# The last two blocks' output product by two levels of seven products instead of one, in a kernel for linear attention and a gated feed-forward layer

## The chip, the cores and the metric

The kernel runs on one core of one Trainium2 chip. The metric is the device time of one execution in microseconds (us). All data are fp32. TensorE (PE) multiplies, VectorE (DVE), ScalarE (ACT) and GpSimd (POOL) work on what it makes, and SyncE (SP) issues most transfers; ACT issues some too. Each engine runs its own instructions in order and waits for the others on semaphores.

## The reference, cut to what matters

```python
kv  = einsum('bhsd,bhse->bhde', k, v)           # 8 batches, 8 heads, 576 positions, 64 wide
att = einsum('bhsd,bhde->bhse', q, kv)
x   = att / sqrt(mean(att**2) + 1e-6) * g_norm  # then (4608 tokens) x 512
g   = x @ w_gate                                # 512 x 1536
h   = silu(g) * (x @ w_val)                     # 4608 x 1536
out = h @ w_out                                 # 1536 x 512
```

The change is in the last line, for the last 1024 of the 4608 tokens. The feed-forward layer takes nearly all of TensorE's time.

## The kernel before, in words

The tokens are cut into nine blocks of 512, numbered 0 to 8. Block 0's products are plain. Blocks 1 and 2 use one level of a scheme that multiplies two matrices of 2x2 parts with seven products of parts and some sums (the Winograd form). Blocks 3 to 8 go in pairs: `Pair.up` makes h for two blocks at once, with two levels of the scheme, so with 49 products of sixteenths (`Inner`). `Ffn.down` then makes the output of one block at a time, with one level (`Down`).

**The up stage of a pair** walks over six units `j`, each of 256 columns of h for gate and value. A unit has four groups of the seven outer products: `GROUPS = ((1, 5), (6, 2), (7,), (4, 3))`; every group runs the seven inner products in the order 1, 5, (3 of the last group), 6, (4 of the last group), 2, 7. A product is one matmul of 128x128 weights by 256 columns for each outer product of its group. Products 1, 6, 7 and 4 of a group add up in one `b` bank of PSUM, 5 and 3 in a `c` bank, 2 stands in the one `a` bank. After each product its bank is read into SBUF (an eviction): by ACT for products 1, 5, 6 and 4 of the first group (L830), else by VectorE, which adds a running sum (L130). Product 6 may only write onto `b` when product 1's eviction has read it, and so on. When product 4 of the fourth group has been evicted, `made3` multiplies h: two `128x1024` multiplies (L132) on GpSimd (on VectorE for the last unit), with a Silu on ACT between (L862). Then `Ffn.h_sums` makes, for block 7 alone, two `128x256` sums for the down stage on the same engine. GpSimd also makes sums for the running `shared[2]` (`made1`, `made2`).

**The weights' parts** for the up stage lie in DRAM (`stream.dram`) and are loaded by SP (L906) into a pool of nine `t` tiles, each time when one comes free (`Stream.pump`).

**The down stage of a block** has seven products of twelve matmuls, `h` as the stationary operand (128x128) and 256 columns of `wo` moving. The order is 1, 5, 6, 2, 7, 3, 4 for the last pair's blocks (`lone`). Sums over `wo` (`turn_t`) are made by GpSimd into `t` tiles. Product 3 of block 8, the last, is split over two `m` banks, so that the other half can be stored while its last half runs (`third`).

**What sets the order.** A scheduler places each engine's instructions by dependency and its own estimate of when each can start; an instruction may so stand earlier in the built order than in the text. `with in_order(engines)` keeps the text's order on the named engines. `tc.issue_after` holds an instruction behind another. Transfers are told done through eight semaphores taken in turn by all transfers of SP and ACT (lanes); a transfer on a lane is issued when the lane's previous one has landed.

Of the kernel before, what the change touches and what calls it, by code (L numbers as in the profile page):

```python
# [14 lines left out]
P = 128  # L15
# [3 lines left out]
def kernel(  # L19
# [620 lines left out]
    class Quad:  # L640


        def __init__(self, steps):
            self.steps = steps
            self.ps, self.room = {}, None

            self.apart = {}

        def prepare(self):
            pass  # L650

        def multiply(self, p):
            name, first = CHAIN[p]
            if first:
                tiles = [PSUMS[name].tile([P, 2, HB], F32, name=name) for _ in range(1 + (name in self.apart))]
                self.ps[name], self.apart[name] = tiles[0], tiles[-1]
            banks = self.ps[name], self.apart[name]
            for e, i in self.order(p):
                lhsT, rhs = self.operands(p, e, i)

                self.ffn.multiplied = nc.tensor.matmul(  # L661
                    banks[e][:, e], lhsT=lhsT, rhs=rhs, start=first and i == 0 and (e == 0 or banks[0] is not banks[1]),
                    stop=i == self.steps - 1, skip_group_check=True,
                )
            getattr(self, f"after{p}", lambda: None)()
# [91 lines left out]
    class Inner:  # L757
# [94 lines left out]
        def made3(self, p, e, q):  # L852
            if p != 4:
                return
            h = h_both[:, :, 2 * self.j : 2 * self.j + 2]
            halves = lambda t: t.rearrange("p (b e) t -> p b e t", b=2)
            c11, c12, c21, c22 = (self.whole(*i) for i in ((1, 1), (3, 1), (3, 0), (1, 0)))

            engine = nc.gpsimd if self.j + 1 < NP else nc.vector
            mul(engine, h[:, :, :, 0:HB], halves(c11), halves(c12))  # L860
            with tc.issue_after(self.ffn.fifth.ins):
                nc.scalar.activation(out=c21, in_=c21, func=ACT.Silu)  # L862
            mul(engine, h[:, :, :, HB:BLK], halves(c21), halves(c22))
            self.ffn.ended = self.ffn.a.h_sums(self.j, 1, engine)

    OUTERS, INNERS = (1, 5, 6, 2, 7, 4, 3), (1, 6, 2, 3, 7, 4, 5)
# [12 lines left out]
    class Stream:  # L879
# [15 lines left out]
        def pump(self):  # L895

            while self.next and not self.held[-9]:
                n, j, c = key = self.next.pop(0)
                tile_ = t_tile(key)
                os, ps = JOINT[c]  # L900
                count = len(os) * len(ps)
# [4 lines left out]
                nc.sync.dma_start(out=to, in_=src)  # L906

        def use(self, n, j, o, p):
            c, i = self.joint[o, p]
            key = n, j, c  # L910
            self.uses[key] -= 1
            if not self.uses[key]:
                self.free(key)
            return self.tiles[key][:, i]
# [70 lines left out]
    class Down(Quad):  # L985
        def __init__(self, ffn):
            super().__init__(NP)
            self.ffn = ffn
            self.t = {}
            self.final = ffn.n == NB - 1  # L990
            self.lone = False
            self.opens = None
            self.keeps = False
            if self.final:
                self.apart["c"] = None

# [14 lines left out]

        def multiply(self, p, es=(0, 1)):
            if p == 3 and self.lone:
                self.third(es)
                return
            super().multiply(p)
# [5 lines left out]

        def third(self, es):


            if es[0] == 0:
                tiles = [m_psum.tile([P, 2, HB], F32, name="m") for _ in range(1 + self.final)]
                self.thirds = tiles[0], tiles[-1]
            for e in es:
                for i in range(self.steps):  # L1030
                    lhsT, rhs = self.operands(3, e, i)
                    self.ffn.multiplied = nc.tensor.matmul(  # L1032
                        self.thirds[e][:, e], lhsT=lhsT, rhs=rhs, start=i == 0 and (e == 0 or self.final),
                        stop=i == self.steps - 1, skip_group_check=True,
                    )
            if not self.final:
                add(nc.vector, self.o1[:, :, HD:DM], self.thirds[0], self.u2)
                self.ffn.store(self.o1, 0)
                return
            for e in es:  # L1040
                add(nc.vector, self.o1[:, e, HD:DM], self.thirds[e][:, e], self.u2[:, e])
                self.ffn.store(self.o1[:, e : e + 1, HD:DM], e, slice(HD, DM))

        def after6(self):
            super().after6()
            if self.lone:
                self.add_c(self.u2, self.u2)

        def order(self, p):
            order = [(e, i) for e in range(2) for i in range(self.steps)]  # L1050
            return order if p == 3 and self.final else sorted(order, key=lambda ei: ei[1])

# [15 lines left out]

        def rows(self):
            o = ring()  # L1070
            self.o1, self.o2 = o[:, 0:2], o[:, 2:4]

        def after2(self):
            if self.lone:
                self.rows()
            add(nc.vector, self.o1[:, :, 0:HD], self.ps["a"], self.s)
            if self.final:
                self.ffn.store(self.o1[:, :, 0:HD], 0, slice(0, HD))

# [3 lines left out]
        def after7(self):  # L1083
            if not self.lone:
                self.rows()
            u3 = self.piece(2)
            nc.scalar.copy(out=u3, in_=self.ps["b"])
            self.add_c(self.o2[:, :, HD:DM], u3)

# [4 lines left out]
        def after3(self):  # L1094
            self.add_c(self.o1[:, :, HD:DM], self.u2)
            if not self.final:
                self.ffn.store(self.o1, 0)
                return
            for e in range(2):
                self.ffn.store(self.o1[:, e : e + 1, HD:DM], e, slice(HD, DM))  # L1100

        def add_c(self, o, u):

            if not self.final:
                add(nc.vector, o, self.ps["c"], u)
                return
            for e, c in enumerate((self.ps["c"], self.apart["c"])):
                add(nc.vector, o[:, e], c[:, e], u[:, e])

    class Ffn:  # L1110
# [8 lines left out]

        def store(self, o, t, columns=slice(None)):  # L1120
            rows = out[BLK * self.n : BLK * (self.n + 1), columns].rearrange("(t p) d -> p t d", t=T)
            nc.sync.dma_start(out=rows[:, t : t + o.shape[1], :], in_=o)
# [39 lines left out]
        def down(self, nxt, then={}):  # L1162

            down = self.down_
            fill = nxt.steps() if nxt else {}
            down.lone = nxt is None
            order = (1, 6, 5, 7, 2, 4, 3) if 5 in fill else (1, 5, 6, 7, 2, 4, 3)
            if down.lone:
                order = (1, 5, 6, 2, 7, 3, 4)
            for p in order:  # L1170
                if p == 1 and 7 not in down.t:
# [4 lines left out]
                with tc.issue_after(nxt.multiplied.ins) if self.n == 0 and p in (5, 6) else ExitStack():  # L1176
                    down.multiply(p, *[(0,)] * (p == 3 and down.lone and down.final))
                self.make(12)
# [9 lines left out]
                if p == 1:  # L1188

                    with tc.issue_after(nxt.q_turned.ins) if self.n == 0 else ExitStack():  # L1190
                        down.turn_s3()
            if down.lone and down.final:
                down.multiply(3, (1,))

# [24 lines left out]
    class Pair:  # L1219


        def __init__(self, n):
            self.n = n
            self.a, self.b = (Ffn(i, blocks[i]) for i in (n, n + 1))
            self.visited = None

        def up(self, fill):

            a = self.a
            a.s1 = s_pool.tile([P, NP, HB], F32, name="s1")  # L1230
            units = []
            for j in range(NP):
# [3 lines left out]
            for i, this in enumerate(units):  # L1236
                for unit, p in this.sequence(last):
                    if unit:
                        visited, self.visited = self.visited, None
                        with tc.issue_after(visited.ins) if visited else ExitStack():  # L1240
                            unit.multiply(p)
                last = this
                fill.get(i + 1, lambda: None)()
            a.down_ = Down(a)
            a.down_.keeps = True
            a.down_.turn_t(5)
            for unit, p in last.sequence(None):
                if unit is None:
                    last.multiply(p)
            a.ended = self.ended  # L1250

# [164 lines left out]
    for n in range(PAIRED, NB, 2):  # L1416
# [3 lines left out]
        if after:  # L1420
# [10 lines left out]
            for i in range(8):  # L1431
                fill[12 + i] = lambda i=i, after=after: after[i // 4].load_quarters(i % 4 // 2, (i % 2,))
        pair.up(fill)
        if after:
            after[0].turn()
        if len(after) > 2:
            after[2].load_kv(0)
        with in_order(nc.tensor.engine):
            pair.a.down(after[0] if after else None, {5: pair.second_sums})
            if after:  # L1440
                after[1].turn()
            if len(after) > 2:
                after[2].load_kv(1)
            pair.b.down(after[1] if after else None)

# [30 lines left out]
```

## Time and profile before

| | |
|---|---|
| median of 3 runs | 1013.08 us (1012.63 to 1014.5) |
| the profiled execution's own time | 1012.7 us |
| its span in the profile | 1010.9 us |
| granted TensorE clock | 1.0 |
| PE, DVE, POOL, ACT busy | 98%, 67%, 37%, 23% of the span |
| first matmul of the up stage of blocks 7 and 8 | 807.6 us |
| its last matmul, and first of the down stage | about 935 us |
| last matmul of the kernel | ends at about 1007.5 us |

A line of a group gives line of the kernel, engine, operation, tiles written and read, shapes, count, then busy time in us and mean in ns of one, then the engine's idle time just before and what ended it. A line of a timeline gives the start in us, the time that the merged instructions took, engine, line and operation, count, and in brackets the idle time before. In the table of stretches each engine's busy us stands with its count in brackets: PE, PE's weight loads, DVE, ACT, POOL, then clock, DMA share and GB/s. L130, L131 and L132 are the helpers `add`, `sub` and `mul`, so their users are told apart by tiles: `wo`, `arena` (x and h), `s`, `t`, `ld`, `r` are in SBUF, `a`, `b`, `c`, `m` in PSUM.

### The profile page before, as it was taken

What the parts mean: (1) busy time and instruction counts of PE and PEld (TensorE: products, weight loads), DVE (VectorE), ACT (ScalarE), POOL (GpSimd) and SP (SyncE); (2) the same over time, 40 slices, a digit from 0 to 9 for tenths busy, and PEclk for the clock granted to TensorE, in tenths of its full rate; (3) what the DMA queues carried; (4) which work ended last, traced back from release to release, by engine and by line L of the source; (5) the groups of instructions that cost most, each with busy time, mean ns of one, the idle gap of its engine ahead of it and who ended that gap; (6) DMA issues with size and microseconds to landing.
All of it is one profiled execution on the core that took longest, in us unless ns stands there. A gap on an engine that the chain in (4) does not pass through costs nothing.

```text
span 1010.9 us, 17078 instructions
## 1 busy us (share of the span) xinstructions
PE 993.7 (98%) x6506; PEld 831.6 (82%) x6506; DVE 673.7 (67%) x1121; ACT 232.2 (23%) x367; POOL 369.6 (37%) x290
## 2 busy tenths in 40 slices
PE   5999999999999999999999999999999999999998
PEld 4544688888888888888888888888888888888887
DVE  2999797589868477656676746666668566666311
ACT  2665111221122311212211121121112121121000
POOL 0000263255544240445456004455660026546600
PEclk9999999999999999999999999999999999999999
DMA  8688653483866855767742464667221654553011
GB/s 220 198 266 260 120 93 136 97 288 97 210 136 122 214 114 158 189 179 182 170 130 42 111 164 135 182 164 191 77 42 43 146 164 144 150 145 101 1 42 42
DMA packets 254290, 143.23 MB, mean 142 GB/s; under 512 B 149504, under 2 KB 236544, under 8 KB 254208
## 3 DMA queue, kind: packets, MB, share of 16 engines
q1 hardware_dynamic: 223488, 138.20, 50.8%
q10 hardware_dynamic: 30656, 3.94, 2.5%
q8 instruction: 52, 0.85, 0.4%
q14 instruction: 30, 0.25, 0.1%
q0 software_dynamic: 64, 0.00, 0.0%
HBM read 104.99 MB, written 28.70 MB: 132 GB/s over the span
## 4 chain that ended last, share of the span: by engine, by line
PE 75%; DMA 1%; POOL 0%; SPq 0%; issue 0%; DVE 0%; POOLq 0%
PE b L816 22%; PE b L661 20%; PE c L816 11%; PE c L661 9%; PE a L816 5%; PE a L661 5%; PE m L431 1%; PE m L1032 1%; PE m L370 1%; DMA ld<-in_v_dram 1%; POOL t L131 0%; SPq L312 0%; PE b L370 0%; PE b L431 0%; PE a L431 0%
## 5 line engine op out<-in xcount | busy, mean ns | idle before, releaser
L816 PE MATMUL b<-arena,t 128*128 128x256 f32 x1008 | 244.5, 381 | 0.0
L816 PEld LDWEIGHTS b<-arena,t 128*128 128x128 f32 x1008 | 190.1, 190 | 29.6 <-DVE r L130 2.4
L130 POOL TENSOR_TENSOR r<-r 128x256 f32<-128x256 f32 (+1 forms) x90 | 94.7, 1054 | 246.1 <-DVE r L130 154.9
L130 DVE TENSOR_TENSOR r<-b,r 128x512 f32<-128x512 f32 (+1 forms) x234 | 138.9, 606 | 60.1 <-PE b L816 54.8
L130 DVE TENSOR_TENSOR r<-c,r 128x512 f32<-128x512 f32 (+1 forms) x170 | 104.5, 623 | 81.9 <-PE c L816 40.1
L132 POOL TENSOR_TENSOR arena<-r 128x1024 f32<-128x1024 f32 (+1 forms) x54 | 102.1, 1904 | 112.3 <-DVE r L130 67.9
L131 POOL TENSOR_TENSOR t<-wo 128x512 f32<-128x512 f32 x54 | 76.9, 1445 | 167.8 <-DVE wo L130 105.9
L130 DVE TENSOR_TENSOR r<-a,r 128x512 f32<-128x512 f32 x93 | 59.2, 636 | 108.3 <-PE a L661 70.7
L816 PE MATMUL c<-arena,t 128*128 128x256 f32 x504 | 122.5, 379 | 0.0
L131 DVE TENSOR_TENSOR arena<-arena 128x512 f32<-128x512 f32 (+3 forms) x96 | 104.3, 1101 | 20.0 <-PE b L661 17.7
L816 PEld LDWEIGHTS c<-arena,t 128*128 128x128 f32 x504 | 95.6, 190 | 13.5 <-issue 0.3
L661 PE MATMUL b<-wo,arena 128*128 128x256 f32 x432 | 98.1, 382 | 0.2
L661 PE MATMUL b<-t,arena 128*128 128x256 f32 x432 | 96.2, 379 | 0.0
L661 PEld LDWEIGHTS b<-wo,arena 128*128 128x128 f32 x432 | 81.2, 190 | 12.5 <-DVE arena L132 0.9
L661 PEld LDWEIGHTS b<-t,arena 128*128 128x128 f32 x432 | 82.1, 190 | 11.2
L830 ACT COPY r<-b 128x512 f32<-128x512 f32 x54 | 31.7, 586 | 189.9 <-PE b L816 189.9
L131 POOL TENSOR_TENSOR t<-arena 128x512 f32<-128x512 f32 x36 | 51.1, 1432 | 56.2 <-PE c L661 21.9
L816 PE MATMUL a<-arena,t 128*128 128x256 f32 x252 | 66.1, 379 | 0.0
L816 PEld LDWEIGHTS a<-arena,t 128*128 128x128 f32 x252 | 47.9, 190 | 6.5
L661 PE MATMUL c<-t,s 128*128 128x256 f32 x216 | 48.1, 379 | 0.0
L661 PE MATMUL a<-wo,arena 128*128 128x256 f32 x216 | 48.1, 379 | 0.0
L661 PEld LDWEIGHTS a<-wo,arena 128*128 128x128 f32 x216 | 41.0, 190 | 5.6
(115 smaller groups left out, 1242.9 us busy)
## 6 DMA issues: line engine op xcount, KB each, us to landing
t<-w SPq DMA_DIRECT2D x180, 256.0 KB, 3.1
out_dram<-r SPq DMA_DIRECT2D x17, 512.0 KB, 2.9
ld<-in_k_dram SPq DMA_DIRECT2D x26, 288.0 KB, 4.6
ld<-in_v_dram SPq DMA_DIRECT2D x26, 288.0 KB, 6.1
t<-w SPq DMA_DIRECT2D x54, 128.0 KB, 2.3
ld<-in_moe_w_gate_dram SPq DMA_DIRECT2D x12, 512.0 KB, 4.6
ld<-in_moe_w_val_dram SPq DMA_DIRECT2D x12, 512.0 KB, 4.7
ld<-in_moe_w_out_dram SPq DMA_DIRECT2D x12, 512.0 KB, 4.8
```

What stands on the lines that cost most here:

```text
L130: add = lambda e, o, a, b: e.tensor_tensor(out=o, in0=a, in1=b, op=OP.add)
L131: sub = lambda e, o, a, b: e.tensor_tensor(out=o, in0=a, in1=b, op=OP.subtract)
L132: mul = lambda e, o, a, b: e.tensor_tensor(out=o, in0=a, in1=b, op=OP.mult)
L370: self.positions = nc.tensor.matmul(self.kv_ps[r][u * D : (u + 1) * D, g, :], lhsT=k[:, u, c, :], rhs=v[:, u, c, :], start=(c == 0), stop= ...
L431: self.multiplied = nc.tensor.matmul(self.ps[i][u][p : p + D, t, j, :], lhsT=self.qt[rows, tile_t, head, p : p + D], rhs=kvs[b % 3][rows, ...
L661: self.ffn.multiplied = nc.tensor.matmul(banks[e][:, e], lhsT=lhsT, rhs=rhs, start=first and i == 0 and (e == 0 or banks[0] is not banks[1 ...
L816: self.ffn.multiplied = nc.tensor.matmul(ps[:, i], lhsT=stream.use(self.ffn.n, self.j, o, p), rhs=self.operand(o, p), start=first and i == ...
L830: copied = nc.scalar.copy(out=dst, in_=ps)
L1032: self.ffn.multiplied = nc.tensor.matmul(self.thirds[e][:, e], lhsT=lhsT, rhs=rhs, start=i == 0 and (e == 0 or self.final), stop=i == self ...
```

## The change

Blocks 7 and 8 go down together, by two levels of seven products. `w_out` is cut into 4x4 parts (3 x 128 rows, 128 columns), h of both blocks likewise (per part 3 x 128 columns of h by 128 tokens of each block). There are 49 products of three matmuls. The weights' part (128x128) is now the stationary operand and h moves, 256 columns; the result has output columns on the partitions and tokens along the rows, so it is turned before it is stored: two quarters by VectorE in blocks of 32x32, put in place by sends of 32 x 8 x 32 elements (16 issued by ACT, 16 by SP), two by 16 transposes on TensorE.

In the up stage of the last pair, `tick` runs one step of a list on every second product: 6 sums over `wo` in place (128x512), 12 sums into the four `ld` tiles (128x384), and nine times three sums through the `s` tile (128x512, 128x128, 128x256) and a store of 448 KB to DRAM by SP. The down stage loads 21 tiles of 192 KB back. GpSimd's two sums behind h's multiplies take both blocks (128x512 each). VectorE's inner sums over h (`turn`) for units 0-1 and 2-3 are put into a list with a due time, 16 products after h is made; those of units 4-5 are made in the down stage. The down stage's text is written out product by product in `Deep.down`, under `in_order` for TensorE and VectorE. `lone`, `third`, `add_c` and block 8's second accumulation bank fall away.

```diff
+    class Last(Inner):
+        GROUPS = ((1, 2), (6, 5), (7,), (4, 3))
...
+        def multiply(self, p, cs=(0, 1, 2)):
...
+            for c in cs:
+                for i, o in enumerate(self.outers):
+                    self.ffn.multiplied = nc.tensor.matmul(
+                        ps[:, i], lhsT=self.deep.weight(o, p, c), rhs=self.deep.operand(o, p, c),
+                        start=first and c == 0 and i == 0, stop=c == 2, skip_group_check=True,
+                    )
+            stream.pump()
...
+            if p in self.ADDED:
+                add(nc.vector, dst, ps, dst)
+            elif self.g == 3:
+                add(nc.vector, dst, ps, self.shared[2][:, :, :, e, q])
+            elif self.g == 0:
+                nc.scalar.copy(out=dst, in_=ps)
+            else:
+                add(nc.vector, dst[:, 0], ps[:, 0], self.onto[:, :, e, q])
+                if n > 1:
+                    nc.scalar.copy(out=dst[:, 1], in_=ps[:, 1])
+    class Deep:
...
+        def prepare(self, temp):
...
+                self.later += [
+                    lambda t=t, b22=b22: sub(nc.vector, t, b22, t), lambda t=t, b11=b11: add(nc.vector, t, t, b11)
+                ]
...
+                        lambda o=o, b=b, x=x, k=k, n=n: sub(
+                            nc.vector, self.kept[o][:, x], b[:, :, k, n], b[:, :, 0, 1]
+                        )
...
+                    self.later += [
+                        lambda b=b, rows=rows, raw=raw: sub(nc.vector, raw, b[:, rows], self.quadrant(6)[:, rows]),
+                        lambda: sub(nc.vector, temp[:, 4], temp[:, 0], temp[:, 1]),
+                        lambda: sub(
+                            nc.vector, temp[:, 5:7], temp[:, 2:4], temp[:, 1:2].to_broadcast([P, 2, P])
+                        ),
+                        lambda i=i, c=c: nc.sync.dma_start(out=self.dram[:, i, c], in_=temp[:, 0:7]),
+                        None, None,
+                    ]
+        def tick(self):
+            self.count += 1
+            if self.count % 2 == 0:
+                if self.due and self.due[0][0] <= self.count:
+                    self.due.pop(0)[1]()
+                    return
+                step = self.later.pop(0) if self.later else None
+                if step:
+                    step()
+        def made(self, j, engine, c21, g, v, h):
+            def second():
+                mul(engine, h[:, :, :, HB:BLK], g, v)
+                a11, a21, a22 = h[:, :, 0, 0:HB], h[:, :, 0, HB:BLK], h[:, :, 1, HB:BLK]
+                add(engine, a21, a21, a22)
+                sub(engine, a21, a21, a11)
...
+            second()
+            if j % 2:
+                self.due += [(self.count + 16, step) for step in self.turn(j // 2, (0, 1))]
+        def turn(self, c, halves):
...
+            return [lambda: add(nc.vector, a21, a21, a22), lambda: sub(nc.vector, a21, a21, a11)]
+        def turn_back(self, e, q, final=False):
+            ps = m_psum.tile([P, 2, 2, P], F32, name="m")
+            for o in range(2):
+                for f in range(2):
+                    nc.tensor.transpose(ps[:, o, f], self.shared[3][:, o, f, e, q], ident)
+            to = self.rows[:, e, q]
+            if final:
+                nc.vector.tensor_copy(out=to[:, 0], in_=ps[:, 0])
+                nc.scalar.copy(out=to[:, 1], in_=ps[:, 1])
+            else:
+                nc.scalar.copy(out=to, in_=ps)
...
+                queue = nc.scalar if final and o else nc.sync
+                queue.dma_start(out=blocks_[row : row + P, :, col : col + P], in_=to[:, o])
+        def down(self):
...
+            m(0, 7)
+            self.outer(5, ((0, 0), (0, 1)))
+            m(0, 3)
+            m(1, 1)
+            self.sum_x(0, 6, 5)
+            m(0, 4)
...
+            add(nc.vector, c11, p1, c11)
+            m(2, 4)
+            nc.vector.transpose(out=room[:, 0], in_=c11)
+            self.send(room[:, 0], 0, 0, nc.scalar)
+            m(3, 6)
+            add(nc.vector, c22, u3, c22)
+            m(3, 5)
+            nc.vector.transpose(out=room[:, 1], in_=c22)
+            self.send(room[:, 1], 1, 1, nc.sync)
+            m(3, 2)
+            m(3, 7)
...
+            self.turn_back(0, 0)
+            m(3, 3)
+            self.turn_back(1, 1)
+            m(3, 4)
+            self.turn_back(1, 0)
+            self.turn_back(0, 1, True)
...
+        if pair.deep:
+            stream.leaves(pair.deep)
+            pair.up(fill)
+            with in_order(nc.tensor.engine, nc.vector.engine):
+                pair.deep.down()
+            continue
```

`sum_x(x, o)` makes one inner sum of h for outer product o, `outer(o)` one outer sum of h by quarters; both are `128x768` on VectorE. `m(g, p)` is inner product p of group g.

## The prediction

> **What bounds the kernel now.** I read the page first, then the chain of waits, the timelines of the last 200 us engine by engine, and the groups kept apart by shape.
>
> ```profile
> PE 993.7 (98%) x6506; PEld 831.6 (82%) x6506; DVE 673.7 (67%) x1121; ACT 232.2 (23%) x367; POOL 369.6 (37%) x290
> ```
>
> TensorE is busy 98% of the span. The chain's last pieces (start, length, what) and PE's timeline show that nothing holds it at the end:
>
> ```profile
> 935.02 5.18 PE b L661 x24
> ...
> 1004.95 2.60 PE m L1032 x12
> 1007.55 0.02 issue
> 1007.58 0.42 DVE r L130
> ```
>
> Blocks 7 and 8 go down from 935.02 to 1007.55: 14 products of 5.18 us, 24 records each, so 215.9 ns a record and 431.8 ns a matmul (the trace shows two records for each fp32 matmul). Before that their six units of h take 127.3 us, 21.16 us each. The stretches of 21 us there show PE busy without a break, VectorE 14.16, GpSimd about 11.3 us:
>
> ```profile
> 850.00:871.00 21.00, 21.00 (x100) 18.47 (x99) 14.16 (x24) 4.31 (x7) 11.29 (x9) 1.00 0.51 151
> ```
>
> So a matmul less is worth its full time only if VectorE and GpSimd, which the change loads, release PE no later than now. VectorE's timeline at the fifth unit's end shows how close that is:
>
> ```profile
> 916.36 0.69 DVE L130 TENSOR_TENSOR r<-b,r 128x512 f32<-128x512 f32 x1 [1.09 <-PE b L816]
> ...
> 919.76 0.69 DVE L130 TENSOR_TENSOR r<-c,r 128x512 f32<-128x512 f32 x1
> 920.62 0.69 DVE L130 TENSOR_TENSOR r<-c,r 128x512 f32<-128x512 f32 x1 [0.17 <-PE c L816]
> 921.48 0.69 DVE L130 TENSOR_TENSOR r<-b,r 128x512 f32<-128x512 f32 x1 [0.17 <-PE b L816]
> ```
>
> Where all seven evictions of a group are VectorE's, one of 0.69 us comes every 0.86 us; 0.17 us is spare. A product that adds onto a bank waits for that bank's last eviction, with two products (1.7 us) between. GpSimd at the same place, and PE:
>
> ```profile
> 917.20 4.69 POOL L132 TENSOR_TENSOR arena<-r 128x1024 f32<-128x1024 f32 x2 [3.80 <-DVE r L130]
> 921.97 0.73 POOL L130 TENSOR_TENSOR s<-arena 128x256 f32<-128x256 f32 x1
> ```
> ```profile
> 923.01 1.46 PE L816 MATMUL b<-arena,t 128*128 128x256 f32 x6
> ```
>
> And an early stretch, in which both engines add with all operands in SBUF:
>
> ```profile
> 173.98 1.27 POOL L132 TENSOR_TENSOR arena<-r 128x512 f32<-128x512 f32 x1
> 175.21 1.45 POOL L131 TENSOR_TENSOR t<-arena 128x512 f32<-128x512 f32 x1
> ```
> ```profile
> 172.46 0.69 DVE L130 TENSOR_TENSOR r<-c,r 128x512 f32<-128x512 f32 x1 [0.79 <-PE c L661]
> 174.16 1.37 DVE L131 TENSOR_TENSOR arena<-arena 128x256 f32<-128x256 f32 x1 [1.00 <-DMA w<-arena]
> ```
>
> VectorE's 128x256 takes 0.42 us alone. Started at 174.16, inside GpSimd's add that ends at 175.25, it ends at 175.53, 0.28 us behind it; GpSimd's next, 1.27 alone, takes 1.45. The eviction at 172.46 reads PSUM and keeps its 0.69 us under GpSimd.
>
> [...]
>
> **The change part by part.**
>
> *Products.* Two blocks of 7x12 are 168 matmuls; 7x7 products of 3 are 147, with the same 128x256 size. 21 x 0.4318 = **-9.1 us**. Weights and h change sides; a weight load stays 128x128, 190 ns under a 216 ns record.
>
> *Transposes.* 16 of 128x128; L494 issues such every 109 ns. **+1.7 us** on PE.
>
> *h's inner basis.* The sums over h of units 0-1 and 2-3 stand 16 products later in the written text. The built order, which a scheduler makes, has them elsewhere: VectorE's first sum stands right behind the eviction of product 3 of the first group of the next unit, 5 products behind the eviction that lets GpSimd multiply h, and it waits for GpSimd. Read it off the lines above, which are this place one unit on: GpSimd multiplies until 921.89, then makes two sums, now 128x512 in place of 128x256 since both blocks have them (1.27 each, as such sums take at 948-955): 924.4. VectorE would begin its sum at 921.3: it stands 3.1 us. The sum (128x1024, 1.22) ends at 925.7, the eviction of product 6, queued behind it, at 926.3; PE's product 7, at 923.0 now, waits for that: 3.3 us. Walked with all small gaps it is 2.9 at each of the two places, with 0.8 and 0.1 for the second sum, and 0.6 for delays of the densest added sums: **+7.4 us**. Units 4-5 are turned in the down stage, in pieces.
>
> *VectorE's 45 sums over weights in the up stage* (6 of 128x512 over wo, 12 of 128x384, 9 times 128x512, 128x128 and 128x256): 4.1 + 6.7 + 12.6 = 23.4 us, and 4.9 for h's sums, against 128 - 85.4 = 43 us spare in the six stretches. Alone they would fit but for the 0.6 us above. But all have two SBUF inputs, and GpSimd works 58% of the time (11.3 + 1.1 of 21.2), 7.1 us a unit of it in 128x1024 instructions of 2.36. The trace has no VectorE sum under one of these; the bounds are nothing, if they let it through, and 2.36 us each. I take the whole instruction, since the 1.27 us ones hold for all of theirs. Walking the built order of both engines with the rows' durations, nine sums start while GpSimd works: four of them behind a 2.36 us one for about 2 us each, in all 10 us. Where this falls in a group with 0.17 us spare, the evictions behind it pass 1.7 us of lateness and PE waits: 2.7 and 0.5 in unit 1, 1.5 and 0.5 in unit 3, the rest at the h sums: **+5.8 us** (0 to +10).
>
> *VectorE in the down stage*: 33 sums of 128x768 (31.6), 57 us in all under PE's 65.8. In the written order each falls due before its product, one sum deep: no PE wait above 0.1 us when walked. GpSimd is idle there, so nothing holds it. Cover gone, each sum is 0.96 us.
>
> *SP.* Nine stores of 448 KB wait on VectorE's sums, and weight loads queue behind them; nine tiles are in flight, one used every 1.6 us, landing in 3.1, so 4 us of hold reach nobody. 21 loads of 192 KB replace GpSimd's tiles. Sends of 32 KB: 16 on ACT and 16 on SP, 0.45 us an issue as the q loads of L333, 7 us each, done before the last row stores; if they cost 0.8 like L522's, SP runs late by 2 us more.
>
> *The end.* After the last product: VectorE's add (0.8 with its wait), less the 0.4 of transposes done meanwhile: 0.6. After the last transpose VectorE copies (0.43), ACT copies behind it (0.35), ACT stores (1.7 to land). SP's last store waits on the same semaphore lane as ACT's, so it is issued when that has landed: 1.7 more. 4.4 against 2.3 now (0.42, 1.7): **+2.7 us** in all.
>
> Sum: -9.1 + 1.7 + 7.4 + 5.8 + 2.7 = +8.5 us. The profiled execution took 1012.7, 0.4 below the median of 1013.08; on the median that is **1021.5**.
>
> **Rivals.**
> - *Short holds*: 128x1024 multiplies let VectorE through. Then +2.7, **1015.8** (1014.5 to 1018). For: no record shows the hold. Against: every 1.27 us one held.
> - *VectorE the bound*: sums run 5% over the price or holds line up; the walk with 3% more gives +12.5, with 2 us for late sends **1027**.
> - *Faster*: GpSimd is done when VectorE comes to h's sums, and the holds fall in slack: -9.1 + 1.7 + 2.7 = -4.7, **1008.4**. It decides at 3 us: GpSimd would have to end the h sums by 921.3 in the lines above, when its own two multiplies end at 921.89. One of the two waits gone alone gives 1013-1018.
> - *It doesn't do what it says*: the delay of 16 products is in the text, 5 in the built order; that is part of the forecast.
>
> **How the numbers follow.** About 0.2% (2 us) is what a measurement of this kernel can tell from no change. Forecast 0.60 (own range 1018.5 to 1025); short holds 0.22, of which 0.19 lie above 1015.1; VectorE the bound 0.08; within 2 us by a missing wait 0.04; faster 0.06. Slower 0.87, same 0.07, faster 0.06. The range reaches from the short holds to part of the bound: 1014.8 to 1026.5.
>
> **What would show it.** Right: the down stage has 294 product records in about 65 us; VectorE's groups at the h sums show about 3 us each ended by POOL; PE shows gaps of 1.5 to 3 us in units 1 to 4; VectorE's means for wo, ld and s sums lie above 0.69, 0.56, 0.69; the last store is issued 1.7 us after ACT's. Wrong: PE's up stage still 127 us (then 1008), or sums at their own price with PE waiting only at h's sums (1016), or PE waiting in the down stage.

## The result, and the profile after

The changed kernel takes 1025.51 us in the median of four runs (1024.39 to 1026.67) against 1012.86 for the kernel before (four runs): a ratio of 1.0123, 95% interval 1.0106 to 1.0141. That is 12.7 us more, where 8.5 were forecast. The forecast was 1021.5 us, and its own range, 1018.5 to 1025, ends just below the result. The profiled execution took 1025.72 us, with a span of 1023.6 against 1010.9.

The first line of the page, and the stretches (columns as explained above) of the up and the down stage after:

```profile
PE 993.3 (97%) x6480; PEld 827.5 (81%) x6480; DVE 735.2 (72%) x1222; ACT 233.8 (23%) x371; POOL 357.8 (35%) x275
```
```profile
850.00:871.00 21.00, 16.67 (x67) 13.99 (x67) 12.22 (x22) 3.40 (x5) 10.26 (x8) 0.84 0.46 146
...
913.00:935.00 22.00, 17.77 (x74) 14.79 (x75) 14.22 (x24) 3.83 (x5) 8.22 (x8) 0.92 0.37 108
...
951.70:1017.00 65.30, 65.01 (x307) 56.86 (x305) 54.32 (x71) 6.33 (x12) 0.00 (x0) 1.00 0.27 63
```

Where 21 us held 100 records of PE before, they hold 67 now. The granted clock, the column after POOL's, is 0.84 and 0.92 where it was 1.00. In the down stage PE is never idle for long. Measured on PE's records, from the first of one stage to the first of the next, the span splits so:

| | before | after | difference |
|---|---|---|---|
| up stage of blocks 7 and 8 | 127.3 | 144.6 | +17.3 |
| down stage, to PE's last record | 72.7 | 66.1 | -6.6 |
| from there to the end | 3.3 | 5.8 | +2.5 |

What stands before the up stage was 0.5 us shorter in the trace after. Of the 17.3 us, 11.9 are stops of PE (times in which it has no record running) and some 4 are records that ran slower than 216 ns right behind two of these stops; the rest, about 1.4, are short delays that I did not split. The stops are 1.0 (unit 1), 4.3 (unit 2), 0.7 and 1.4 (unit 3), 4.3 and 0.2 (unit 4). This is PE's timeline at the second long one, at h's inner sums of units 2 and 3:

```profile
912.15 0.59 PE L813 MATMUL b<-arena,t 128*128 128x256 f32 x2
917.03 1.53 PE L813 MATMUL c<-arena,t 128*128 128x256 f32 x4 [4.28 <-DVE r L130]
918.76 2.07 PE L813 MATMUL b<-arena,t 128*128 128x256 f32 x4 [0.20 <-DVE r L130]
...
924.31 1.46 PE L813 MATMUL c<-arena,t 128*128 128x256 f32 x6
```

Four records take 1.53 and 2.07 us behind the stop, while six take 1.46 a few us later. VectorE's timeline there, with GpSimd's and SP's below it, tells why PE stood:

```profile
905.19 0.69 DVE L131 TENSOR_TENSOR s<-wo 128x512 f32<-128x512 f32 x1 [3.39 <-DMA leaf<-s]
...
909.33 0.68 DVE L130 TENSOR_TENSOR r<-c,r 128x512 f32<-128x512 f32 x1
915.15 1.23 DVE L130 TENSOR_TENSOR arena<-arena 128x1024 f32<-128x1024 f32 x1 [5.15 <-POOL arena L131]
916.29 0.68 DVE L130 TENSOR_TENSOR r<-c,r 128x512 f32<-128x512 f32 x1
```
```profile
907.76 4.68 POOL L132 TENSOR_TENSOR arena<-r 128x1024 f32<-128x1024 f32 x2 [5.10 <-DVE r L130]
912.51 1.26 POOL L130 TENSOR_TENSOR arena<-arena 128x512 f32<-128x512 f32 x1
913.85 1.26 POOL L131 TENSOR_TENSOR arena<-arena 128x512 f32<-128x512 f32 x1
```
```profile
893.76 6.05 SPq L1207 DMA_DIRECT2D t<-w  x6
900.21 0.33 SPq L962 DMA_DIRECT2D leaf<-s  x1
```

Read from below: a leaf piece is what three of VectorE's sums make in `s` and one store of 448 KB takes to DRAM, nine times in all. VectorE had ended one at 898.07. Its store stood on SP behind weight loads that waited for `t` tiles, was issued 2.1 us later and landed at 905.2. Three of the nine stores went so, issued 2.0 to 2.6 us late and landing 4.0 to 6.2 us after that; they are the three long waits of VectorE, 3.0, 4.3 and 3.4 us. The next sum goes into the same `s` tile; VectorE waited 3.39 us for it, with evictions behind it. So GpSimd's multiplies, which need those evictions, started late; h's inner sum, which VectorE meets a few instructions on, waited 5.15 us for GpSimd's second sum; PE waited for the eviction behind that. The table of waits of the up stage has both (what waits, us in all, times, longest):

```profile
DVE s L131 <- DMA leaf<-s: 12.1, 6, 4.3
...
DVE arena L130 <- POOL arena L131: 8.9, 2, 5.1
```

The end, from the row stores' own view (line, queue, count, then ns of an issue as minimum, median and maximum, and the first and last start in us). PE's last record ends at 1017.8:

```profile
L1082 SPq DMA_DIRECT2D out_dram<-r x7: 372/435/490, 1014.9 to 1020.6; - x7
...
L1082 ACTq DMA_DIRECT2D out_dram<-r x1: 399/399/399, 1018.7 to 1018.7; - x1
```

SP's last store is issued at 1020.6, when ACT's of 1018.7 has landed (1.8 us from issue to landing).

### The profile page after: what moved, and what is told of

Its sections match the earlier page's. It is cut to its first block, busy times and chain, and to the rows that moved or that the text cites. A ratio compares the mean times of both kernels' runs of the same rounds, so it can differ in the third digit from the quotient of the medians.

```text
span 1023.6 us, 17215 instructions
## 1 busy us (share of the span) xinstructions
PE 993.3 (97%) x6480; PEld 827.5 (81%) x6480; DVE 735.2 (72%) x1222; ACT 233.8 (23%) x371; POOL 357.8 (35%) x275
## 4 chain that ended last, share of the span: by engine, by line
PE 70%; DMA 3%; DVE 1%; POOL 1%; issue 1%; SPq 0%; ACT 0%; DVEq 0%; POOLq 0%
PE b L813 19%; PE b L658 16%; PE c L813 9%; PE c L658 8%; PE a L813 5%; PE a L658 4%; PE b L889 4%; PE c L889 2%; DMA t<-w 1%; PE m L431 1%; DVE r L130 1%; PE a L889 1%; PE m L370 1%; POOL arena L132 1%; DMA leaf<-s 1%
## 5 line engine op out<-in xcount | busy, mean ns | idle before, releaser
L813 PE MATMUL b<-arena,t 128*128 128x256 f32 x1008 | 247.5, 384 | 8.2 <-DVE r L130 7.7
L130 DVE TENSOR_TENSOR r<-b,r 128x512 f32<-128x512 f32 (+1 forms) x247 | 145.2, 601 | 58.0 <-PE b L813 47.2
L131 DVE TENSOR_TENSOR arena<-arena 128x512 f32<-128x512 f32 (+5 forms) x119 | 121.8, 1040 | 9.2 <-PE b L658 6.9
L131 POOL TENSOR_TENSOR t<-wo 128x512 f32<-128x512 f32 x45 | 64.2, 1450 | 162.9 <-DVE wo L130 103.4
L658 PE MATMUL b<-wo,arena 128*128 128x256 f32 x336 | 76.8, 382 | 0.2
L658 PE MATMUL b<-t,arena 128*128 128x256 f32 x336 | 74.8, 379 | 0.0
L658 PEld LDWEIGHTS b<-wo,arena 128*128 128x128 f32 x336 | 62.9, 190 | 10.0 <-DVE arena L132 0.9
L658 PEld LDWEIGHTS b<-t,arena 128*128 128x128 f32 x336 | 63.8, 190 | 8.7
L813 PE MATMUL a<-arena,t 128*128 128x256 f32 x252 | 66.1, 379 | 0.0
L130 DVE TENSOR_TENSOR arena<-arena 128x512 f32<-128x512 f32 (+4 forms) x46 | 39.9, 883 | 9.3 <-POOL arena L131 8.9
L658 PE MATMUL b<-arena 128*128 128x256 f32 x192 | 45.5, 380 | 0.0
L658 PE MATMUL b<-arena,t 128*128 128x256 f32 x192 | 45.4, 379 | 0.0
```

The lines of the kernel that those rows point to most:

```text
L130: add = lambda e, o, a, b: e.tensor_tensor(out=o, in0=a, in1=b, op=OP.add)
L131: sub = lambda e, o, a, b: e.tensor_tensor(out=o, in0=a, in1=b, op=OP.subtract)
L658: self.ffn.multiplied = nc.tensor.matmul(ps[:, e], lhsT=lhsT, rhs=rhs, start=first and i == 0 and e == 0, stop=i == self.steps - 1, skip_g ...
L813: self.ffn.multiplied = nc.tensor.matmul(ps[:, i], lhsT=stream.use(self.ffn.n, self.j, o, p), rhs=self.operand(o, p), start=first and i == ...
```

## The experiments

Three theories stood against each other. **Stores**: VectorE waits for the leaf store before and everything follows. **GpSimd**: h's inner sums stand on VectorE ahead of evictions while GpSimd is not done. **Holds**, the prediction's: sums with two SBUF inputs wait out the GpSimd instruction they fall under. The scheduler answers every edit with another order, so the first kernel fixes the order, and the next ones move one thing in it.

**VectorE's order fixed as built** (`e1`)

```diff
-                    if deep:
-                        deep.tick()
+        SUMS = [0, 0, 0, 0, 0, 0, 2, 5, 6, 6, 7, 10, 11, 18, 21, 22, 22, 22, 22, 23, 23, 27, 29, 30, 35, 40, 40,
+                46, 47, 47, 51, 59, 64, 70, 71, 71, 75, 77, 78, 83, 88, 88, 94, 95, 95]
+        TURNS = [53, 54, 100, 101]
+        def evicted(self):
+            self.count += 1
+            while self.SUMS and self.SUMS[0] <= self.count:
+                self.SUMS.pop(0)
+                self.later.pop(0)()
...
+            with in_order(nc.vector.engine):
+                pair.up(fill)
```

The numbers count VectorE's evictions in the up stage, 24 a unit; `SUMS` places the 45 sums over weights, `TURNS` h's four.

> VectorE's added sums of the up stage are put by hand behind the same evictions behind which the built program of the changed kernel has them, and its order there is fixed; nothing else changes. It is the base of the next three. Every theory expects the time of the changed kernel, 1025.5 within 2 us, with PE gaps of some 4 us at each of the two places of h's inner sums, about 12 us of VectorE waiting for leaf stores and 9 us waiting for GpSimd's sums.

1022.3 us (1021.12 to 1023.97), ratio 1.0099 (1.0078 to 1.0119): not the base that I expected. The median is 3.2 us under the changed kernel's, 2.7 when each is set against the kernel before in its own runs, and the two intervals overlap; in the traces the up stage is 2.4 us shorter. The waits of its up stage, and its SP queue at the place shown above:

```profile
DVE arena L130 <- POOL arena L131: 5.5, 2, 4.2
DVE s L131 <- DMA leaf<-s: 2.6, 5, 1.1
```
```profile
892.22 4.24 SPq L1220 DMA_DIRECT2D t<-w  x3
896.56 0.42 SPq L966 DMA_DIRECT2D leaf<-s  x1
897.07 6.28 SPq L1220 DMA_DIRECT2D t<-w  x6
```

VectorE's order is the same, apart from a few of the first sums and one eviction; SP's has changed. The store of the piece ended at 896.53 goes at once, with three loads ahead of it and the others behind, and VectorE's wait for stores falls from 12.1 to 2.6 us. The stops at h's sums are 3.2 and 2.9 us in place of 4.3 and 4.3 + 0.2. So the store theory fits the difference of 2 to 3 us, by the place of the store in SP's queue. As SP's order changed without being set by the edit, this is read from the trace, not shown by an edit of its own.

**A second room for the leaf pieces** (`e2`), on the base:

```diff
-                    raw = temp[:, 0:4].rearrange("p (k n) d -> p k (n d)", k=2)
+                    odd = (3 * i + c) % 2
+                    t = temp[:, 7:12] if odd else temp[:, 0:5]
+                    u = kvs[0].rearrange("p s d -> p (s d)").rearrange("p (n d) -> p n d", n=2) if odd else temp[:, 5:7]
+                    raw = t[:, 0:4].rearrange("p (k n) d -> p k (n d)", k=2)
```

> As the base, but every other leaf piece is made in a second room, so that a sum does not wait for the store of the piece before. VectorE's order is the same; each store is two DMAs. Store theory (VectorE stands for the leaf store before, which makes its evictions, then GpSimd's multiplies, then h's sums and PE late): VectorE's 12 us of waiting for stores go, the PE gaps of 0.7 and 1.4 us of unit 3 go, those at h's sums shrink from 4.3 to about 3 us, and the clock keeps up better after them: 6 to 9 us off, 1017 to 1019. GpSimd theory alone (h's sums stand ahead of evictions, whatever the stores do): at most 2 us off, 1023.5 or more. Hold theory of the prediction (VectorE's two-input sums wait out GpSimd's instructions, the stores ride along): within 2 us of the base too, since every sum and every GpSimd instruction is still there.

1022.86 us, ratio 1.0106 (1.0091 to 1.0122): no gain on the base. The waits for stores are gone from the trace, but the stops at h's sums are what they were, 3.2 and 2.9 us. The first sums of the leaf pieces show why, in the changed kernel, the base and here (busy us, mean ns, then the idle time before):

```profile
L131 DVE TENSOR_TENSOR s<-wo 128x512 f32<-128x512 f32 x9 | 6.6, 728 | 12.1 <-DMA leaf<-s 12.1
```
```profile
L131 DVE TENSOR_TENSOR s<-wo 128x512 f32<-128x512 f32 x9 | 10.9, 1209 | 2.6 <-DMA leaf<-s 2.6
```
```profile
L131 DVE TENSOR_TENSOR s<-wo 128x512 f32<-128x512 f32 x9 | 13.5, 1497 | 0.0
```

Waiting and working together are 18.7, 13.5 and 13.5 us. From the base to here the wait for stores only turned into longer sums: a sum that need not wait for a store starts sooner and takes longer, up to 2.87 us, under GpSimd's multiplies. So the two causes can stand in for each other, and VectorE's 12.1 us of waiting for stores cost it 5.2 us net. As a theory of the whole loss, the stores have fallen.

**h's inner sums later** (`e3`), and **both** (`e4`):

```diff
-        TURNS = [53, 54, 100, 101]
+        TURNS = [62, 64, 110, 112]
```

> As the base, but h's four inner sums stand where the text's count of 16 products puts them, 8 to 11 evictions later; one leaf room as in the changed kernel. GpSimd theory: VectorE's 9 us of waiting for GpSimd go, the two PE gaps of 4.3 us and the slower clock behind them go: 10 to 13 us off, 1013 to 1016. Store theory: the late VectorE still holds PE behind the leaf stores, gaps of 1.5 to 2.5 us stay in each of units 2 to 4: 5 to 8 us off, 1018 to 1020. Hold theory: at most 3 us off, 1022 or more.

1015.6 us, ratio 1.0033 (1.0022 to 1.0045): 6.7 us off the base, and no wait of VectorE for GpSimd is left. In the trace the up stage is 9.1 us shorter than the base's: 4.5 of stops, 4.3 of slow records. Stops of 1.2, 1.3 and 1.6 us stay, with no slow record behind any of them.

> Second room and h's sums late together. If stores and h's sums are the whole loss in the up stage, PE shows no gap over 1.5 us there and the 16.6 us that the up stage lost shrink to under 4: 1010 to 1012.5. Hold theory: GpSimd's instructions still hold the sums, 8 us or more of the loss stay: 1017 or more.

1013.91 us, ratio 1.0012 (1.0004 to 1.0019). With h's sums out of the way the second room is worth 1.7 us: the stop of 1.6 falls to 0.3. The up stage is 131.8 us, so 4.5 of the 17.3 are left, where the expectation gave under 4 without holds and 8 or more with them: neither. What holds it is seen on VectorE and GpSimd, here at the stop of 1.3 us:

```profile
857.38 0.69 DVE L130 TENSOR_TENSOR r<-b,r 128x512 f32<-128x512 f32 x1 [0.16 <-PE b L813]
857.99 2.87 DVE L131 TENSOR_TENSOR s<-wo 128x512 f32<-128x512 f32 x1
860.78 1.28 DVE L130 TENSOR_TENSOR r<-c,r 128x512 f32<-128x512 f32 x2
```
```profile
855.64 4.67 POOL L132 TENSOR_TENSOR arena<-r 128x1024 f32<-128x1024 f32 x2 [3.67 <-DVE r L130]
```

The sum costs 0.69 alone. It started at the beginning of the second multiply and took 2.87: it waited out 2.2 us of GpSimd, and the two evictions behind it came late.

**The same sums where GpSimd is idle** (`e5`):

```diff
-        SUMS = [... 18, 21, 22, 22, 22, 22, 23, 23, 27, 29, 30, 35, 40, 40, 46, 47, 47, ...]
+        SUMS = [... 17, 18, 19, 23, 24, 41, 42, 43, 47, 47, 48, 65, 66, 67, 71, 71, 72, ...]
...
-                queue = nc.scalar if final and o else nc.sync
+                queue = nc.sync
```

> As the run with second room and h's sums late, but the 27 leaf sums and the last five sums over wo stand behind other evictions: those after which GpSimd has nothing to do (17 to 19 and 23 to 24 of each unit's 24). The number and size of the sums are the same. Besides, both last row stores leave from SP's queue. Hold theory (a sum with two SBUF inputs waits out the GpSimd instruction it falls under, and that is what the 1.2 and 1.3 us gaps are): no gap over 0.3 us in the up stage, its length 128 to 129.5 against 131.8; with 1.6 us from the end, 1008 to 1009.5, under the kernel before. Rival, VectorE's sheer load (23 us of sums in 43 us spare): gaps of 3 us in all stay, 1011 to 1012.5.

1009.07 us (ten runs, 1007.05 to 1010.99) against 1012.25 before, ratio 0.9973 (0.9963 to 0.9983): faster than both kernels. The up stage takes 128.9 us and shows no stop over 0.1. The groups by shape of the leaf sums, first of `e4`, then of `e5` (busy us, mean ns), and one stretch of `e5`:

```profile
L131 DVE TENSOR_TENSOR s<-wo 128x512 f32<-128x512 f32 x9 | 11.4, 1269 | 0.0
L131 DVE TENSOR_TENSOR s<-s 128x128 f32<-128x128 f32 x9 | 4.4, 493 | 0.0
```
```profile
L131 DVE TENSOR_TENSOR s<-wo 128x512 f32<-128x512 f32 x9 | 6.5, 728 | 0.0
...
L131 DVE TENSOR_TENSOR s<-s 128x128 f32<-128x128 f32 x9 | 2.6, 285 | 0.1
```
```profile
850.00:871.00 21.00, 20.94 (x97) 17.89 (x95) 16.95 (x29) 4.66 (x7) 11.01 (x9) 1.00 0.63 189
```

The same nine sums cost 6.5 us in place of 11.4. The work is all there (VectorE is busy 16.95 of the 21 us), so VectorE's load as such was no bound.

**GpSimd's instructions in halves** (`e6`), with the sums where `e4` has them:

```diff
-            mul(engine, h[:, :, :, 0:HB], halves(c11), halves(c12))
+                for b in range(2):
+                    mul(engine, h[:, b, :, 0:HB], halves(c11)[:, b], halves(c12)[:, b])
```

> As the run with second room and h's sums late, with VectorE's sums at the same places, but GpSimd's 128x1024 instructions of these units (two multiplies and one sum a unit) are each made in two of 128x512; both last row stores leave from SP's queue. Hold theory: a sum waits at most 1.3 us in place of 2.4, the sum that took 2.87 us takes under 2, and the gap of 1.3 us in unit 2 goes; the one of 1.2 in unit 1 shrinks by a few tenths: 1010 to 1011.5 with 1.6 from the end. If the hold is not for one instruction but for a stretch of GpSimd work, the gaps stay and only the 1.6 us of the end show: 1012 to 1012.6.

1010.45 us, ratio 0.9981 (0.9973 to 0.999). The sum that took 2.87 us slips between two multiplies and takes 0.71; the stop of 1.3 us is gone, that of 1.2 is 0.9, and one of 0.7 appears in unit 3. The up stage takes 130.3 us where `e4` has 131.8, with every sum of VectorE's in its place. So the hold is for one instruction and its length counts, but the means of the leaf sums stay high (1104 and 542 ns).

**Stops of known size in the kernel before** (`e7`), for the slow records:

```diff
                     add(nc.vector, dst, ps, self.onto(e, q))
+                    if self.ffn.n + 2 == NB and self.g == 1 and p == 5:
+                        for _ in range((8, 10, 12, 15, 20, 30)[self.j]):
+                            nc.vector.tensor_copy(out=kvs[0], in_=kvs[1])
```

> The kernel before, with VectorE's order fixed as written in the last two blocks' six units and useless copies of 128x256 put into VectorE behind one eviction of each unit: 8, 10, 12, 15, 20 and 30. They make PE stand for times from nothing to some 10 us. Clock theory: where PE stands under about 2 us, its records go on at 216 ns; above about 3 us the clock granted falls to half for about 5 us afterwards, and 2 to 2.5 us are lost after each such stop, however long it was. Rivals: the loss grows with the stop; or the records keep 216 ns, and what looked like a slower clock was waiting.

The kernel ran once, in 1046.07 us. The 8 copies made no stop; the others gave stops of 2.6, 2.3, 2.9, 4.5 and 9.7 us. PE's timeline at the first and at the longest:

```profile
841.83 1.13 PE L816 MATMUL c<-arena,t 128*128 128x256 f32 x4 [2.55 <-DVE r L130]
842.79 1.03 PE L816 MATMUL b<-arena,t 128*128 128x256 f32 x4
...
955.77 1.22 PE L816 MATMUL c<-arena,t 128*128 128x256 f32 x2 [9.70 <-DVE r L130]
956.79 1.91 PE L816 MATMUL b<-arena,t 128*128 128x256 f32 x4
```

Behind the stop of 2.55 us four records take 1.03 us as ever; behind 9.7 they take 1.91, with 427 ns from one to the next in the trace, for 3 to 4 us. The loss hardly grows with the stop: 1.5 us behind 2.3, 1.8 behind 2.9 and 4.5, 2.6 behind 9.7.

**The last store from SP's queue** (`e8`), the second edit of `e5` alone on the changed kernel:

> The changed kernel, with one edit: the last of the row stores, which left from ACT's queue, leaves from SP's, after the other. The lane theory of the prediction (SP's last store is issued only when ACT's has landed): the two are issued 0.5 us apart, the stretch from PE's last record to the end shrinks from 5.8 to about 4.2 us, 1023.8. If the end is set by the landing of the stores themselves, it stays at 1025.5 or becomes longer by one issue, 0.4 us.

1025.01 us (1022.01 to 1027.05), ratio 1.0138 (1.0122 to 1.0155): in the median it can't be told from the changed kernel. In the trace the stretch from PE's last record to the end is 4.1 us in place of 5.8, and SP issues its last stores 0.54 us apart (view of the row stores):

```profile
L1082 SPq DMA_DIRECT2D out_dram<-r x8: 372/438/490, 1012.6 to 1016.6; - x8
```

The lane wait is shown. These four runs, 5 us apart, can't show the gain of 1.7 us, but the traces do: the stretch from PE's last record to the end is 5.8 to 6.9 us in the six with ACT's store last (the changed kernel, `e1` to `e4`, `e10`) and 4.1 to 5.1 us in the four with SP's (`e5`, `e6`, `e8`, `e9`).

**h's sums early, and nothing else** (`e9`): `e5` with `TURNS = [53, 54, 100, 101]`.

> The fastest kernel so far (sums in GpSimd's gaps, second room, both last stores from SP), with one edit: h's four inner sums stand where the changed kernel has them, 8 to 11 evictions earlier. No leaf sum or store is late there, so this prices the step of the prediction by itself. The prediction's walk (VectorE waits some 3 us for GpSimd at each of two places, no clock): PE gaps of 2.9 and 2.9 + 0.8 us, 7.4 us more, 1016.5. With the clock theory each of the two stops costs another 2.2 us: about 11 us more, 1020. If the waits were bred by late evictions only, GpSimd is done in time here and it stays under 1012.

1016.65 us, ratio 1.0053 (1.0033 to 1.0074). The median is 7.6 us above that of `e5`, 8.3 when each is set against the kernel before in its own runs, and the traces' up stages are 7.5 us apart (136.4 and 128.9). PE's timeline at both places:

```profile
863.14 1.13 PE L813 MATMUL b<-arena,t 128*128 128x256 f32 x4 [2.93 <-DVE r L130]
...
908.88 1.25 PE L813 MATMUL c<-arena,t 128*128 128x256 f32 x4 [2.93 <-DVE r L130]
910.61 2.08 PE L813 MATMUL b<-arena,t 128*128 128x256 f32 x4 [0.48 <-DVE r L130]
```

The stops are the walk's, 2.9 and 2.9 + 0.5. Only the second is followed by slow records (1.3 us), so the total is 6.3 us of stops and these 1.3, near the walk's 7.4 and below what I expected with the clock.

**The text's order kept** (`e10`): the changed kernel with `with in_order(nc.vector.engine):` around `pair.up(fill)`.

> The changed kernel, with one edit: VectorE's order in the up stage is kept as the text has it. So h's sums really come 16 products later and the sums over wo are spread one to two products. GpSimd theory with the clock: no wait of VectorE for GpSimd, no stop of PE over 2 us, no loss of clock; held sums leave many stops of up to 1.3 us, 8 to 10 us in all: 1016 to 1019. If the delay in the text is no better than the built order, 1024 or more.

1018.9 us, ratio 1.0071 (1.0052 to 1.009). Twelve stops, none over 1.0 us, 6.5 in all, no wait of VectorE for GpSimd's sums, none for the leaf stores, and no slow records behind the longer stops. The up stage takes 137.4 us, 7.2 less than in the built order. The 16 products of the text do what they say once the scheduler may not undo them; how much of the gain is theirs, and how much that of the stores, this run does not part. The sums, spread evenly, still fall under GpSimd: the 128x384 ones take 883 ns in the mean, the 128x256 ones 830, where the same shapes take 550 and 416 in `e5`.

## Why the prediction was right, and where its terms were not

- *Products and transposes, -9.1 + 1.7, and 0.6 before the last transposes*: -6.8 forecast, -6.6 measured. VectorE was said to keep up in the down stage with 57 us of work; it is busy 54.3 of 65.3 and PE's only wait there is 0.44 us, ahead of the last transposes. The prediction's 0.96 and 0.56 us for sums of 768 and 384 columns were my estimates; a line through 691 ns for 512 columns and 1090 for 896, both in the trace of the kernel before, gives 957 and 558. The 768 ones took 948 to 950 ns in the changed kernel's down stage, the 384 ones 550 in `e5`.
- *h's inner basis, +7.4*: right as a step. `e9` has the stops of the walk, 6.3 us; that its up stage comes to 7.5 is partly luck, for 1.3 of it are slow records, which the walk left out. In the changed kernel the two stops were 4.3 and 4.5, since GpSimd started late.
- *Holds, +5.8 (0 to +10)*: the wait is shown (2.87 us for a sum of 0.69 in `e4`), the size and place were not. From `e4` to `e5` they are worth 2.9 us of the up stage, and `e6` gets 1.5 of it by shorter instructions alone. In the changed kernel itself VectorE's leaf and `ld` sums cost some 5 us more than alone (x9 of 494 against 285 ns, and so on), not the 10 of the walk: VectorE stood for stores first, and its sums came later. In `e2`, where it never stands for a store, the first sums alone cost 7.3 us more than alone at 0.69 us each. The stop of 2.7 in unit 1 was 1.0.
- *SP, "4 us of hold reach nobody"*: this is the step that failed. It asked who waits behind the stores on SP, the weight loads, and not who waits for the stores: the next sum into the one `s` tile. 12.1 us of VectorE's time went there, 5.2 net of the holds that take their place, worth 2 to 3 us in the end (`e1`); what is left in the base is worth nothing with h's sums early (`e2`), and 1.7 us with them late (`e3` to `e4`).
- *Clock*: no step had it. Some 4 us of the changed kernel are slow records behind the two long stops, about as much as the forecast of the up stage (13.2) is short of the measured 17.3. That the stops themselves come near the forecast, 11.9 us, is partly luck: less hold, more store.
- *The end, +2.1 behind the last transposes*: +2.5, by the lane, as written.
- *The sum*: 1013.08 + 8.5 is 1021.6, not 1021.5, and the rival with 12.5 + 2 comes to 1027.6, not 1027; neither changes anything.

So the direction and the kinds of wait were right, and the size 4 us short. Of the signs named for being right, the 294 records of the down stage in 66 us and the late last store came. The stops did not come as named: they are 0.7 to 1.4 and twice 4.3 us, not 1.5 to 3; VectorE's two waits for GpSimd are 3.8 and 5.1 us, not 3; and the sums over `wo` in place keep 0.68 us.

The rivals: short holds is refuted, for a hold of a whole multiply stands in `e4`'s trace, 2.87 us for 0.69. VectorE's load as the bound is refuted by `e5`. The faster case named its condition well, GpSimd done when VectorE comes to h's sums and the added sums in slack; `e5` meets both by placing the same work, with the second room and the end of `e8` besides, at 1009.07 where the rival said 1008.4.

## What to carry to other kernels

Ask of a new store not only what queues behind it but which buffer it keeps, and who writes there next. Added work on an engine with time to spare is free only in places: place it where the engine whose instructions it was seen to wait out is idle (nine of VectorE's sums took 11.4 us in `e4`, some of them under GpSimd's instructions, and 6.5 in `e5`, in GpSimd's gaps), and fix the order, since a scheduler pulls it forward to where it can start. Price a stop of TensorE of about 2 us or more with the slower clock that may follow: here it cost 1.4 to 3.1 us where it came.

## What the runs showed of the hardware

- Over the up stages of all twelve traces, 22 stops of PE of 0.7 to 1.61 us were followed by no slow record; of seven between 2.3 and 2.95 us five were; all eight from 3.2 to 9.7 us were. The loss was 1.4 to 3.1 us each, at 427 ns a record in place of 216, over 3 to 6 us. The traces also hold the granted clock itself: its stretches between two changes are multiples of 3.413 us. In the changed kernel it is 0.50 for 6.83 us from 863.0, 2 us into the first long stop, and for 3.41 us from 917.6, just behind the second, with 47.79 us at 1.00 between them and 98.99 after: 2, 1, 14 and 29 times 3.413. Cut into such windows, the up stages part sharply. All 13 windows at full clock in which PE stood for 1.80 us or more were followed by one at half the clock, and none of the other 445, in which it stood for 1.76 us at most (the ends of PE's records are modelled, so the last hundredths are not sure). The two stops of 2.93 us of `e9` lie on both sides of this edge (the clock is the number behind POOL's count):

```profile
858.56:861.97 3.41, 1.65 (x8) 1.12 (x6) 0.71 (x1) 0.58 (x1) 2.53 (x2) 1.00 0.69 221
861.97:865.39 3.42, 2.25 (x10) 1.82 (x10) 3.42 (x6) 0.00 (x0) 0.49 (x1) 1.00 0.00 0
906.34:909.76 3.42, 0.88 (x4) 0.68 (x4) 2.76 (x3) 0.00 (x0) 0.63 (x1) 1.00 0.20 65
909.76:913.17 3.41, 2.93 (x8) 2.11 (x7) 1.84 (x4) 0.00 (x0) 0.72 (x1) 0.50 0.00 0
```

  The first stop is parted by the edge of a window into 1.76 and 1.17 us; of the second, 2.54 us fall into one window, and the next is at half the clock. By this, an estimate from these figures, a stop under 1.76 us would leave the clock alone, one over twice that, 3.5 us, would always halve it, and between them the place of the window would decide.
- In `e4` a VectorE sum with two SBUF inputs that started with a 128x1024 GpSimd multiply waited out the whole of it: 2.87 us for 0.69. The wait for the instruction it falls under, which the prediction had seen under 1.27 us ones only, was so there under one of 2.34 us too. Evictions, which have one input in PSUM, kept their time under such multiplies: 0.69 us at 857.38 in `e4`, 0.68 at 909.33 in the changed kernel.
